# Delta-rule attention ahead of an expert layer and a spectral mixer: loads planned by bytes, zeroing by DMA, filler products and a new order

## The chip, the cores and the metric

The kernel runs on one core of a Trainium2 chip. The metric is the device time of one execution in microseconds (us); the median of three runs is given. The engines are TensorE (PE, whose weight loads are listed as PEld), VectorE (DVE), ScalarE (ACT), GpSimd (POOL) and SyncE (SP), which here only issues transfers. Every engine works through its own instructions in the order of the program and waits at semaphores for the others.

## What is computed

Three layers follow each other for 2 batches of 768 tokens. The first is a recurrent attention (delta rule) with 8 heads of 48 values; its state is updated token by token:

```python
for t in range(S):
    y[:, :, t] = np.einsum('bhd,bhde->bhe', q[:, :, t], state)
    v_old = np.einsum('bhde,bhd->bhe', state, kt)
    state = state + bt[:, :, :, None] * np.einsum('bhd,bhe->bhde', kt, vt - v_old)
```

Here `kt` is the key divided by its norm. The second layer sends each token through one of 8 experts (384 to 1024 to 384 values), chosen by its logits and a local gate. The third adds the real part of a two-dimensional Fourier transform, normalizes, and adds a two-layer network (384 to 1536 to 384). Results have to be close to fp32, so most products are made from fp16 pairs (a high part and a low part), three products for one.

## The kernel before, in words

The program has four stretches: attention (`Attn.run`), routing (`Rest.route`), the experts (`moe_main`) and the mixer. Only the first is touched. `consts_attn` gives it one packed tensor of constants, `ca`.

**Attention.** The 768 tokens are cut into 24 chunks of 32, and 4 chunks make a part `hf` (0 to 5); two parts make a group `g` (0 to 2). For each part there are: `prepK` (L284), which scales the keys by their norms (L291), splits them into a high and a low fp16 buffer (`parts`, L214: L224 on ACT, L243 on DVE or L234 to L238 on PE and ACT), transposes both (`turn`, L164: on PE with a copy by ACT or DVE, or by a DMA), copies the transposed keys into stacked form (`stack`, L313, four copies per part by DVE or ACT as the table `SA` says) and multiplies keys by keys (`gram`, L331); `prepT` (L399) splits the group's solved matrix, spreads it into the block buffers TB (L359 or L362) and multiplies it by the keys (products `wps`, evicted at L421 and L423); `prepV` (L426) splits the values; `prepQ` (L442) splits and spreads the queries (L457, L459, four copies at L466), multiplies them by the keys, masks them (L483) and spreads the result into the block buffers MB. For each group `solve` (L364) inverts a triangular matrix on DVE alone: a stream transpose (L380), 31 pairs of dependent steps (L389, L391) and a transpose of the result, PT (L395). `chain` (L506) carries the recurrent state through the 24 chunks, once for each of two halves of the heads; a step takes products on PE, an eviction on ACT (L531), the low part on DVE or ACT (`low`, L553), the state's eviction on ACT (L548) and its low part `sl` on DVE (`state`, L570). `out` (L576) makes the output of a chunk, `logits` (L620) and `logits_end` (L639) the router's logits from it. When the last parts are ready, `rest` (L670) frees one pool and issues the first expert weights.

**The order.** All of this is written as generators that ask for an engine with a planned time: `yield ("V",929)` asks for DVE for 929 ns. `Order` (L47) is a planner that runs while the program is built. It gives an engine to the request with the smallest priority number (table `PR`, L681; chain and loads have 0) and writes the instructions in that order; `KEEN` and `SHARE` let an engine stay idle a little for an urgent request that is due. Nothing is reordered on the chip. Where two engines can do an operation, `pick` (L59) takes the one that would be done first by the plan, with the corrections of `BIAS` (L680). `dma` (L156) takes SP's queue at 475 ns for an issue, or POOL's at 1081 ns plus `BIAS[6]`, whichever is sooner; in the run shown all loads of attention are issued by SP. `arrive` (L161) says after how many ns from its issue the plan counts a load as landed: a fixed 1850, 2700 or 2900, whatever is queued ahead of it. `LOADS` (L682) is the order of the loads: keys of the first half, constants `c`, `beta`, values, keys of the second half, gate weights `w`, values. The queries' loads (`load_q`, L150) have a priority of their own and fall between them.

**Zeroing.** Twelve fp16 buffers of 128x2048 (QT, TB and MB, two high and two low each) must be zero outside the blocks that are written later, and so must the paddings of the key buffers and the U buffers. `clear` (L195) asks for these as memsets of DVE or POOL (`zero`, L206) with the priorities `CLEAR` (L205).

**TensorE's clock.** `tv` (L491) can put filler products ahead of its own (table `STIRS`, L667), but the table is empty.

Of the kernel before, what the change touches and what calls it, by code (L numbers as in the profile page):

```python
# [6 lines left out]
F32 = mybir.dt.float32  # L7
F32R = mybir.dt.float32r
F16 = mybir.dt.float16
# [13 lines left out]
def consts_attn():  # L23
    c={}
    m=np.zeros((128,32),np.float32)
    for p in range(128): m[p]=(np.arange(32)>(p%32))
    hm=np.zeros((128,2),np.float32)
    for p in range(128): hm[p,(p//32)%2]=SC
    c["ca"]=np.concatenate([hm,m,np.eye(128,dtype=np.float16).view(np.float32),(SC*np.eye(128)).astype(np.float16).view(np.float32),np.eye(128,dtype=np.float32),(-np.eye(128)/SC).astype(np.float16).view(np.float32)],1)
    return c  # L30

def layout(n,a):
# [14 lines left out]
class Order:  # L47
# [3 lines left out]

    LAT={"T":200,"A":160,"V":130,"P":100,"Q":0}
    def __init__(s, keen, share, ticks=None, **res):
        s.KEEN,s.SHARE,s.ticks=keen,share,ticks; s.res=dict(res); s.flags={}; s.wait={}; s.free={}; s.q={}; s.due={}; s.heap=[]; s.n=0; s.now=0
    def add(s,gen,pr=0):
        s.push(s.now,(gen,pr,None))
    def push(s,t,x):
# [6 lines left out]
    def grant(s,e):  # L64

        q=s.q.get(e)
        if not q or s.free.get(e,0)>s.now: return
        pr,_,g,y=q[0]
        s.due[e]=[d for d in s.due.get(e,[]) if d[0]>s.now]
        if any(p<pr and p<=s.KEEN and t<s.now+s.SHARE*y[1] for t,p in s.due[e]): return  # L70
        heapq.heappop(q)
        n=y[1]
        if e=="T" and s.ticks is not None:

            t=(s.now+s.ticks["phase"])//3413; s.ticks[t]=s.ticks.get(t,0)+n
            if s.ticks.get(t-1,0)<1280: n*=2
        s.free[e]=s.now+n
        if "H" in y:

            h=max(s.now,s.free.get("H",0)); s.free["H"]=h+457; s.free[e]+=h-s.now  # L80
        s.push(s.free[e],e)
        s.pr=pr
        n=next(g,None)
        if n is None: return
        t=s.now if 0 in y else s.free[e]+(s.LAT[e] if n[0]!=e or e in "VP" else 0)
        if isinstance(n,tuple) and n[0] in s.LAT: s.due.setdefault(n[0],[]).append((t,pr))
        s.push(t,(g,pr,n))
# [32 lines left out]
class Attn:  # L120
    NB,KP=5,1
    def __init__(s, tc, wk, pk, K, I, q,k,v,beta, xd, lg, psA, psC, psS, late, after):
        s.tc,s.nc,s.wk,s.pk,s.K=tc,tc.nc,wk,pk,K
        s.I,s.lg,s.late,s.after=I,lg,late,after
        s.src={"kp":k,"qp":q,"vp":v}
        s.beta,s.xd=beta,xd
        s.psA,s.psC,s.psS=psA,psC,psS
        s.betaU=pk.tile([128,3,32],F32,name="betaU")
        def zt(n,cnt,sh=[128,16,128],p=wk): return [p.tile(sh,F16,name=f"{n}{i}") for i in range(cnt)]

        s.KBh,s.KBl=[zt(n+"a",1)+zt(n,s.NB-2,p=pk)+zt(n+"b",1) for n in ("KBh","KBl")]
        s.QTs=[zt(f"QT{j}",2) for j in range(2)]
        s.TBh,s.TBl,s.MBh,s.MBl=zt("TBh",2),zt("TBl",2),zt("MBh",2),zt("MBl",2)
        s.Ub=[[zt(f"U{b}{i}",3,[128,2,2,48]) for i in range(2)] for b in range(2)]
        s.L={}; s.KT={}; s.QT={}; s.WT={}; s.V={}; s.G={}; s.P={}; s.PT={}; s.sm={}; s.ST={}
        s.ups=[None]*2; s.S=[None]*2; s.sp={}; s.yb=[None]*2
        s.left={}; s.SB={}; s.STIR=dict(s.STIRS)
        s.o=Order(s.KEEN,s.SHARE,{"phase":0},kp=s.KP,qp=2,vp=1,KT=2,QT0=1,QT1=1,V=2,TB0=1,TB1=1,MB0=1,MB1=1,WT=2,ST=1,ga=2,G=1,P=1,PT=1,SQ=1,am=1,ph=1,u=2,y=2,xT=1,xc=2,yb=3)
    def drop(s,name,key,n=2):

# [3 lines left out]
    def load(s,nm,g):  # L144
        yield ("+",nm)
        t=s.L[nm,g]=s.pk.tile([128,12,4,48],F32,tag=nm,name=nm,bufs=s.KP if nm=="kp" else 1)
        for i in range(3):
            yield from s.dma(t[:,4*i:4*i+4].rearrange("p c q e -> p (c q e)"),s.src[nm][g,:,768*i:768*i+768])
            s.o.add(s.arrive(f"{nm}{3*g+i}",2700))
    def load_q(s):  # L150
        for hf in range(6):
            yield ("+","qp")
            t=s.L["qp",hf]=s.pk.tile([128,1024],F32,tag="qp",name="qp",bufs=2)
            yield from s.dma(t,s.src["qp"][hf])
            s.o.add(s.arrive(f"qp{hf}",2900))
    def dma(s,out,in_,n=475):  # L156

        e=s.o.pick(("Q",n),*(("A",n+35+s.BIAS[5]),)*(s.o.now<s.BOTH),*(("P",1081+s.BIAS[6]),)*(s.o.now<s.THREE))
        yield {"Q":("Q",n,"H"),"A":("A",n+35,"H"),"P":("P",1081)}[e]
        {"Q":s.nc.sync,"A":s.nc.scalar,"P":s.nc.gpsimd}[e].dma_start(out=out,in_=in_)  # L160
    def arrive(s,f,t=1850):  # L161
        yield ("",t)
        yield ("!",f)
    def turn(s,out,in_,f,pe):  # L164

# [18 lines left out]
            yield ("-","y")  # L184
        yield ("!",f)
    def load_beta(s):
        yield from s.dma(s.betaU.rearrange("p g t -> p (g t)"),s.beta)
        s.o.add(s.arrive("beta"))
    def load_consts(s):
        yield from s.dma(s.K["ca"],s.I["ca"])  # L190
        s.o.add(s.arrive("consts"))
    def load_gates(s):
        for t,a in s.late: yield from s.dma(t,a)
        s.o.add(s.arrive("wg"))
    def clear(s):  # L195
        t=s.pk.tile([128,1],F32,tag="one",name="one",bufs=1)
        s.nc.vector.memset(t,1.0)
        s.nc.scalar.activation(out=t,in_=t,func=AF.Sqrt)
        word=lambda t: t.bitcast(F32)
        pad=lambda t: word(t).rearrange("p u (s e) -> p (u s) e",s=2)[:,:,24:32]  # L200
        rows=[(f"K{i}",[pad(s.KBh[i]),pad(s.KBl[i])],(165,260)) for i in range(s.NB)]+[(f"Q{i}",[word(s.QTs[j][i]) for j in range(2)],(912,950)) for i in range(2)]
        rows+=[("U",[t for b in range(2) for i in range(2) for t in s.Ub[b][i]],(107,195))]
        rows+=[(f"{n}{i}",[word(h[i]),word(l[i])],(912,950)) for i in range(2) for n,h,l in (("T",s.TBh,s.TBl),("M",s.MBh,s.MBl))]
        for f,ts,c in rows: s.o.add(s.zero(f,ts,c),s.CLEAR.get(f,9))
    CLEAR={"K0":-1,"K1":0,"Q0":5,"Q1":7,"U":5}  # L205
    def zero(s,f,ts,c):  # L206
        for t in ts:
            e=s.o.pick(("V",c[0]),("P",c[1]))
# [282 lines left out]
    def tv(s,b,c):  # L491
        hf,cc=c//4,c%4; i=hf%2; u0=4*cc+2*b
        if cc==0:
            yield f"V{hf}"
            yield f"T{hf}"
        V=s.V[hf]
        x=s.ups[b]=s.psC.tile([128,2,2,48],F32,tag="u",name="ups",bufs=2)
        for _ in range(s.STIR.pop(c,0)): s.nc.tensor.matmul(out=s.SB[0][:,256:512],lhsT=s.K["identh"],rhs=s.K["idents"],start=False,stop=True,skip_group_check=True)
        yield ("T",255)
        for Q in range(2):  # L500
            u=u0+Q
            s.mm3(x[:,:,Q],[s.TBh[i][:,u],s.TBl[i][:,u]],[V[j][:,u].unsqueeze(1).to_broadcast([128,2,48]) for j in range(2)],Q==0)
        if cc==3:
            yield from s.drop("V",hf)
            yield from s.drop(f"TB{hf%2}",hf)
    def chain(s,b):  # L506
        nc,wk,o=s.nc,s.wk,s.o
# [4 lines left out]
        for c in range(24):  # L512
            hf,cc=c//4,c%4; u0=4*cc+2*b; kb=hf%s.NB
            x=s.ups[b]
# [18 lines left out]
            o.add(s.out(b,c,uh,ul),1)  # L533
            if c<23:
                if c==0:
                    s.SB[b]=s.psS.tile([128,512],F32,tag=f"S{b}",name="S",bufs=1)
                    s.S[b]=s.SB[b][:,0:192].rearrange("p (q a e) -> p q a e",q=2,a=2)
                for n,(st,mv) in enumerate(((s.KBh,uh),(s.KBl,uh),(s.KBh,ul))):
                    if n==0: yield ("T",169)
# [80 lines left out]
    def logits(s,b,hf,yb):  # L620
# [9 lines left out]
        x=s.wk.tile([128,512],F32,tag="xlT",name="xlT",bufs=1)[0:96]  # L630
        yield ("A",478)
        nc.scalar.activation(out=x.rearrange("p (h c t) -> p c h t",h=4,c=4),in_=ps[0:96].rearrange("p (c h t) -> p c h t",h=4,t=32),func=AF.Copy)
        yield ("T",880)
        for h in range(4): nc.tensor.matmul(out=ps[:,0:9],lhsT=x[:,128*h:128*h+128],rhs=s.K["wgq"][:,h],start=(h==0),stop=(h==3))
        yield ("-","xT")
        yield ("A",110)
# [2 lines left out]
    def logits_end(s,b,c,yb):  # L639
# [24 lines left out]
        yield ("!",f"lg{b}{c}")  # L664
        yield ("-","xc")
        yield ("-","ga")
    STIRS={}  # L667
    LOW=(0, 0, 1, 1, 1, 1)
    SA=((0, 0, 0, 0), (0, 0, 0, 0), (0, 1, 1, 0), (0, 1, 0, 1), (1, 0, 0, 0), (0, 0, 1, 1))
    def rest(s):  # L670

        for f in ("ku3","G5","PT2","W43","W53","V4","V5","M4","M5"): yield f
        yield from s.after(s.o)
    BOTH=0
    KEEN,SHARE=2,0.15
    LATE=4
    THREE=30000
    HOLD=(1, 1, 0, 0, 0, 1)
    TK=(1, 1, 0, 0, 0, 0)
    BIAS=(-972, 0, 0, 0, 0, 0, 431, 102)  # L680
    PR={'K0': 0, 'T0': 8.83, 'V0': 28.94, 'Q0': 8.02, 'K1': 4.23, 'T1': 11.55, 'V1': 9.27, 'Q1': 11.93, 'K2': 14.91, 'T2': 2.11, 'V2': 0, 'Q2': 3.47, 'K3': 0.56, 'T3': 11.35, 'V3': 15.56, 'Q3': 8.68, 'K4': 17.19, 'T4': 0, 'V4': 8.5, 'Q4': 9.96, 'K5': 0.49, 'T5': 11.58, 'V5': 7.5, 'Q5': 25.12, 's0': 5.7, 's1': 4.09, 's2': 8.02, 'n0': 1.43, 'n1': 28.97, 'n2': 14.57, 'lq': 7.97, 'lv': 22.18}  # L681
    LOADS="k0 c b v0 k1 w v1"  # L682
    def run(s):
        o=s.o
        s.clear()
        P=lambda n,d: s.PR.get(n,d)
        def loads():
# [863 lines left out]
```

## Time and profile before

| What | us |
|---|---|
| three runs | 580.58, 582.45, 583.3 |
| median | 582.45 |
| the profiled execution | 585.4 |
| its span, first to last instruction | 583.6 |
| DVE busy in the span | 410.7 (70%) |
| PE busy in the span | 490.0 (84%) |

The span is what the profile shows of one execution; 1.8 us of the profiled execution's time lie outside it. Busy shares are means over stretches with different limits, so they are read stretch by stretch: attention runs from 0 to about 244 us, routing to 255, the experts to about 394 and the mixer to the end. The granted clock of TensorE is given as a share of 2.4 GHz; 0.50 is the lower of its two levels.

### The profile page before, as it was taken

To read this page: it belongs to the slowest core of one execution; us is meant where nothing else is said; L and a number is where in the kernel's file an instruction comes from. 1 tells how busy PE (TensorE), PEld (TensorE's weight loads), DVE (VectorE), ACT (ScalarE), POOL (GpSimd) and SP (SyncE) were. 2 spreads that over 40 slices of the span, in tenths; PEclk is the share of its full clock that TensorE was granted. 3 is DMA by queue.
4 is the path that set the end of the run, shared out by engine and by line. 5 is a ranking of instruction groups with operands and counts; after the bars stand their busy time and mean duration, and the time that the engine had idled before them with its cause. 6 is when DMAs were issued, how large, how long until landed. Compare 5 with 4: busy or idle time off the path is not lost.

```text
span 583.6 us, 12586 instructions
## 1 busy us (share of the span) xinstructions
PE 490.0 (84%) x5008; PEld 388.2 (67%) x5008; DVE 410.7 (70%) x918; ACT 332.7 (57%) x769; POOL 77.0 (13%) x81
## 2 busy tenths in 40 slices
PE   0572448884988889769999999999899999999997
PEld 0462147774878778668888888888787655555575
DVE  7969989889994866469888979878987642231132
ACT  3776558995795878836676767672454442111111
POOL 6000000000000000031343322124111210000010
PEclk9986669995895899969999999999999999999999
DMA  7135330766014103829999997328100000010010
GB/s 249 37 51 141 73 73 2 208 98 123 3 28 73 30 2 91 302 60 340 385 323 328 334 300 261 126 67 271 56 2 2 28 1 0 2 55 0 1 55 27
DMA packets 66990, 67.25 MB, mean 115 GB/s; under 512 B 40086, under 2 KB 59483, under 8 KB 66928
## 3 DMA queue, kind: packets, MB, share of 16 engines
q1 hardware_dynamic: 64080, 58.15, 33.4%
q0 software_dynamic: 2848, 8.27, 4.2%
q8 instruction: 40, 0.66, 0.5%
q14 instruction: 22, 0.18, 0.1%
HBM read 51.98 MB, written 7.67 MB: 102 GB/s over the span
## 4 chain that ended last, share of the span: by engine, by line
PE 32%; issue 8%; DVE 7%; DMA 5%; ACT 3%; POOL 1%; SPq 0%; POOLq 0%; ACTq 0%; DVEq 0%
PE mp L1396 12%; PE mop L1422 12%; DMA raw<-moe_w 4%; PE hp L941 3%; DVE ws L917 2%; PE op L953 2%; PE fp L1262 1%; DMA x<-moe_w_ch 1%; PE yp L1231 1%; POOL x2d L962 1%; PE up L1343 1%; ACT ws L914 1%; DVE d L1150 1%; DVE zl L1215 0%; DVE e L1150 0%
## 5 line engine op out<-in xcount | busy, mean ns | idle before, releaser
L1406 DVE SCALAR_TENSOR_TENSOR ml<-mp,mh 128x256 f16<-128x256 f32 (+1 forms) x48 | 26.8, 557 | 81.0 <-ACT mh L1404 80.9
L1396 PE MATMUL mp<-uT,ws 128*128 128x256 f16 (+1 forms) x432 | 77.8, 326 | 0.0
L1422 PE MATMUL mop<-ws,mh 128*128 128x384 f16 x288 | 77.7, 326 | 0.0
L1404 ACT ACTIVATE mh<-mp 128x256 f16<-128x256 f32 (+1 forms) x48 | 23.5, 489 | 89.8 <-PE mp L1396 89.6
L953 PE MATMUL op<-ws,hh 128*128 128x384 f16 (+1 forms) x256 | 67.5, 326 | 0.0
L941 PE MATMUL hp<-xT,ws 128*128 128x240 f16 x576 | 64.8, 266 | 1.0 <-DVE xT L932 0.7
L941 PEld LDWEIGHTS <-ws 128*128 128x128 f16 x576 | 56.2, 98 | 7.2 <-issue 1.5
L1396 PEld LDWEIGHTS <-ws 128*128 128x128 f16 x432 | 42.2, 98 | 27.2
L917 DVE SCALAR_TENSOR_TENSOR ws<-raw,ws 128x1536 f16<-128x1536 f32 x32 | 55.9, 1749 | 0.0
L914 ACT ACTIVATE ws<-raw 128x1536 f16<-128x1536 f32 x32 | 47.3, 1486 | 0.0
L1422 PE MATMUL mop<-ws,ml 128*128 128x384 f16 x144 | 46.9, 326 | 0.0
L953 PE MATMUL op<-ws,hl 128*112 128x384 f16 (+1 forms) x128 | 41.7, 326 | 0.0
L1422 PEld LDWEIGHTS <-mh 128*128 128x128 f16 x288 | 28.2, 98 | 17.8
L330 PEld LDWEIGHTS <-KT 128*128 128x128 f16 x576 | 26.6, 115 | 19.8 <-issue 8.8
L924 POOL DMA_INDIRECT xg<-xd,gm x16 | 22.2, 1389 | 126.8 <-DVE sim L870 120.2
L953 PEld LDWEIGHTS <-hh 128*128 128x128 f16 (+1 forms) x256 | 29.1, 114 | 11.6
L391 DVE TENSOR_TENSOR P<-P,tmp 128x31 f32<-128x31 f32 (+15 forms) x93 | 31.6, 339 | 1.9
L389 DVE TENSOR_TENSOR tmp<-Gu,P 128x31 f32<-128x31 f32 (+15 forms) x93 | 31.3, 336 | 1.9
L962 POOL DMA_INDIRECT x2d<-ot,sim x16 | 19.8, 1238 | 87.5 <-ACT ot L958 85.1
L944 DVE SCALAR_TENSOR_TENSOR hl<-hp,hh 128x480 f16<-128x480 f32 x32 | 20.9, 654 | 14.8 <-ACT hh L943 13.2
L330 PE MATMUL ga<-ST,KT 128*128 128x64 f16 x288 | 16.5, 229 | 17.4 <-DVE ST L326 10.0
L943 ACT ACTIVATE hh<-hp 128x480 f16<-128x480 f32 x32 | 18.1, 567 | 20.6 <-PE hp L941 19.5
(285 smaller groups left out, 1212.4 us busy)
## 6 DMA issues: line engine op xcount, KB each, us to landing
raw<-moe_w SPq DMA_DIRECT2D x64, 384.0 KB
x<-moe_w_ch SPq DMA_DIRECT2D x24, 384.0 KB
qp<-q SPq DMA_DIRECT2D x6, 512.0 KB
kp<-k SPq DMA_DIRECT2D x6, 384.0 KB
vp<-v SPq DMA_DIRECT2D x6, 384.0 KB
xd<-yb SPq DMA_DIRECT2D x48, 48.0 KB
xa<-x2d SPq DMA_DIRECT2D x6, 384.0 KB
ur<-x2d SPq DMA_DIRECT2D x2, 768.0 KB
```

The lines of the kernel that those rows point to most:

```text
L330: s.nc.tensor.matmul(out=out,lhsT=st[l],rhs=mv[m],start=(first and i==0),stop=True,skip_group_check=True)
L389: nc.vector.tensor_tensor(out=x,in0=Gu[:,k,k+1:32].unsqueeze(2).to_broadcast([128,m,n]),in1=P[:,k,0:n].unsqueeze(1).to_broadcast([128,m,n] ...
L391: nc.vector.tensor_tensor(out=P[:,k+1:32,0:n],in0=P[:,k+1:32,0:n],in1=x,op=ALU.subtract)
L914: s.nc.scalar.activation(out=s.W[q][:,0].rearrange("p s c -> p (s c)"),in_=s.raw[q],func=AF.Copy,scale=WS)
L917: s.nc.vector.scalar_tensor_tensor(out=W[1],in0=s.raw[q],scalar=WS,in1=W[0],op0=ALU.mult,op1=ALU.subtract)
L941: nc.tensor.matmul(out=p[:,i],lhsT=s.W[q][:,a,i,128*k:128*k+128],rhs=xT[b][:,k],start=(n==0),stop=(n==8)); n+=1
L953: nc.tensor.matmul(out=s.po[t][0:w],lhsT=hs[a][:,i,128*t:128*t+w],rhs=s.W[q][:,b,i,384:768],start=(g==0 and i==0 and n==0),stop=(g==3 and ...
L962: i=s.nc.gpsimd.indirect_dma_start(out=s.x2d,out_offset=bass.IndirectOffsetOnAxis(ap=s.si[0:w,c:c+1],axis=0),in_=ot,in_offset=None,bounds_ ...
L1396: for k in range(3): nc.tensor.matmul(out=p,lhsT=s.w_ch1(a,k,f),rhs=s.uT[g][b][:,k,0:N],start=(n==0),stop=(n==8)); n+=1
L1404: nc.scalar.activation(out=hh,in_=p,func=AF.Relu)
L1406: nc.vector.scalar_tensor_tensor(out=hl,in0=p,scalar=0.0,in1=hh,op0=ALU.max,op1=ALU.subtract)
L1422: nc.tensor.matmul(out=pm[t],lhsT=hs[a][:,128*t:128*t+128],rhs=s.w_ch2(b,f),start=(f==0 and n==0),stop=(f==11 and n==2))
```

## The change

- A zero tensor of 128x1024 fp32 is a new input. The twelve large buffers (`ZD`) are filled from it by DMA, once the constants have landed by the plan; the paddings and U stay memsets. `CLEAR` has new priorities.
- `arrive` counts a load as landed by bytes: a link that is busy until `s.link` takes 2850 ns per MB, and 1600 ns are added.
- `beta` is loaded ahead of the constants.
- A filler product is a 128x128 by 256-column fp16 product of a zeroed tile `rest0` into an unused half of a PSUM bank. 40 stand ahead of everything, and `STIRS` puts others ahead of PE's turns of the given numbers (a turn is a grant of PE by the plan): 69 in turns 2 to 25, 39 at turn 35, 14 in turns 43 to 78 and 14 in turns 345 to 370. `STIRP` puts 9 products of 128x128 fp32 on PT of group 0 ahead of turn 39.
- `PR`, `KEEN`, `LATE` (the priority of `logits`), `SA` and `BIAS` have new values; `SA` now gives 11 of the 24 stacking copies to ACT (7 before), and `BIAS[6]`, POOL's correction as an issuer of loads, goes from 431 to 0.

```diff
+    c["zero"]=np.zeros((128,1024),np.float32)
...
+        if e=="T":
+            s.turns+=1
+            if s.stir: s.stir(s.turns)
...
-            yield from s.dma(t[:,4*i:4*i+4].rearrange("p c q e -> p (c q e)"),s.src[nm][g,:,768*i:768*i+768])
-            s.o.add(s.arrive(f"{nm}{3*g+i}",2700))
+            yield from s.dma(t[:,4*i:4*i+4].rearrange("p c q e -> p (c q e)"),s.src[nm][g,:,768*i:768*i+768],kb=0.393)
+            s.o.add(s.arrive(f"{nm}{3*g+i}"))
...
+        s.link=max(s.link,s.o.now)+2850*kb
-    def arrive(s,f,t=1850):
-        yield ("",t)
+    def arrive(s,f,t=None):
+        yield ("",s.link-s.o.now+1600 if t is None else t)
         yield ("!",f)
...
-        for f,ts,c in rows: s.o.add(s.zero(f,ts,c),s.CLEAR.get(f,9))
-    CLEAR={"K0":-1,"K1":0,"Q0":5,"Q1":7,"U":5}
+        for f,ts,c in rows: s.o.add(s.zero_dma(f,ts) if f in s.ZD else s.zero(f,ts,c),s.CLEAR.get(f,9))
+    def zero_dma(s,f,ts):
+        yield "consts"
+        for t in ts: yield from s.dma(t.rearrange("p u e -> p (u e)"),s.I["zero"],kb=0.524)
+        s.o.add(s.arrive("0"+f))
+    ZD=("Q0","Q1","M0","M1","T0","T1")
+    CLEAR={'K0': 15.0, 'K1': 13.3, 'Q0': 16.4, 'M0': 20.6, 'Q1': 7.0, 'M1': 0.9, 'U': -0.5, 'K2': 10.9, 'T0': 23.9, 'K3': 22.6, 'K4': 17.6, 'T1': 7.9}
...
-    STIRS={}
+    STIRS={0: 40, 2: 12, 5: 17, 7: 5, 10: 4, 15: 2, 17: 6, 19: 9, 22: 6, 23: 3, 25: 5, 35: 39, 43: 6, 57: 5, 78: 3, 345: 3, 357: 3, 363: 5, 370: 3}
+    def stir(s,k):
+        for _ in range(s.STIRS.get(k,0)):
+            s.nc.tensor.matmul(out=s.SB[0][:,256:512],lhsT=s.rest0[:,0:128],rhs=s.rest0,start=s.fresh,stop=True,skip_group_check=True)
+            s.fresh=False
+        g,n=s.STIRP.get(k,(0,0))
+        if n:
+            x=s.PT[g][:,0:4].rearrange("p a b -> p (a b)")
+            for _ in range(n): s.nc.tensor.matmul(out=s.SB[0][:,256:384],lhsT=x,rhs=x,start=False,stop=True,skip_group_check=True)
+    STIRP={39: (0, 9)}
...
-    SA=((0, 0, 0, 0), (0, 0, 0, 0), (0, 1, 1, 0), (0, 1, 0, 1), (1, 0, 0, 0), (0, 0, 1, 1))
+    SA=((0, 0, 0, 0), (0, 0, 0, 0), (0, 1, 1, 1), (1, 1, 1, 1), (1, 1, 0, 0), (0, 0, 1, 1))
...
-    KEEN,SHARE=2,0.15
-    LATE=4
+    KEEN,SHARE=5,0.15
+    LATE=20
...
-    BIAS=(-972, 0, 0, 0, 0, 0, 431, 102)
-    PR={'K0': 0, 'T0': 8.83, 'V0': 28.94, 'Q0': 8.02, 'K1': 4.23, 'T1': 11.55, 'V1': 9.27, 'Q1': 11.93, 'K2': 14.91, 'T2': 2.11, 'V2': 0, 'Q2': 3.47, 'K3': 0.56, 'T3': 11.35, 'V3': 15.56, 'Q3': 8.68, 'K4': 17.19, 'T4': 0, 'V4': 8.5, 'Q4': 9.96, 'K5': 0.49, 'T5': 11.58, 'V5': 7.5, 'Q5': 25.12, 's0': 5.7, 's1': 4.09, 's2': 8.02, 'n0': 1.43, 'n1': 28.97, 'n2': 14.57, 'lq': 7.97, 'lv': 22.18}
-    LOADS="k0 c b v0 k1 w v1"
+    BIAS=(-972, 0, 970, -319, 0, -211, 0, 287)
+    PR={'K0': 2.56, 'T0': 23.74, 'V0': 19.15, 'Q0': 15.58, 'K1': 6.73, 'T1': 19.9, 'V1': 17.03, 'Q1': 15.71, 'K2': 17.58, 'T2': 4.09, 'V2': 21.01, 'Q2': 7.44, 'K3': 26.4, 'T3': 5.71, 'V3': 8.22, 'Q3': 10.75, 'K4': 40.15, 'T4': 0, 'V4': 16.23, 'Q4': 13.72, 'K5': 3.39, 'T5': 14.94, 'V5': 10.68, 'Q5': 30.12, 's0': 48.55, 's1': 6.77, 's2': 7.72, 'n0': 13.85, 'n1': 13.43, 'n2': 14.57, 'lq': 11.03, 'lv': 8.76}
+    LOADS="k0 b c v0 k1 w v1"
...
+        o.stir=s.stir
+        for b in range(2): s.SB[b]=s.psS.tile([128,512],F32,tag=f"S{b}",name="S",bufs=1)
+        s.rest0=s.pk.tile([128,256],F16,name="rest0")
+        s.nc.gpsimd.memset(s.rest0,0.0)
+        s.stir(0)
         s.clear()
```

## Rows read from the trace of the kernel before

**Rows 1.** The page, part 2: granted clock of TensorE in 40 slices of 14.6 us.

```profile
PEclk9986669995895899969999999999999999999999
```

**Rows 2.** The chain that ended last: start us, us, what (its first piece, its last).

```profile
255.48 1.21 issue
...
579.22 1.05 DVE ur L1430 x2
```

**Rows 3.** Busy time by stretch: us, engines with instructions, PEclk, DMA share, GB/s.

```profile
core 0: us, PE busy (x) PEld busy (x) DVE busy (x) ACT busy (x) POOL busy (x), PEclk, DMA share, GB/s
0.00:78.50 78.50, 31.72 (x365) 24.38 (x366) 67.45 (x163) 46.83 (x75) 9.19 (x23) 0.83 0.45 116
78.50:194.50 116.00, 91.17 (x1476) 83.82 (x1474) 97.56 (x255) 93.62 (x298) 1.90 (x2) 0.82 0.33 67
194.50:244.00 49.50, 44.12 (x769) 40.31 (x765) 29.02 (x81) 40.53 (x144) 0.00 (x0) 0.93 0.35 112
244.00:584.00 340.00, 323.00 (x2414) 239.67 (x2411) 216.61 (x419) 151.72 (x254) 65.93 (x56) 0.98 0.39 132
```

**Rows 4.** DVE in order of time: start us, us, line, operation.

```profile
42.73 1.97 DVE L380 STREAM_TRANSPOSE Gu<-G 128x1024 f32<-128x1024 f32 x1
...
77.23 1.25 DVE L395 STREAM_TRANSPOSE PT<-P 128x1024 f32<-128x1024 f32 x1
...
132.06 1.25 DVE L395 STREAM_TRANSPOSE PT<-P 128x1024 f32<-128x1024 f32 x1
...
193.20 1.25 DVE L395 STREAM_TRANSPOSE PT<-P 128x1024 f32<-128x1024 f32 x1
```

**Rows 5.** All engines in order of time, first 24 us.

```profile
3.10 0.45 SPq L160 DMA_DIRECT2D ca<-ca  x1
...
4.17 0.84 ACT L264 ACTIVATE sq<-kp 128x768 f32<-128x768 f32 x1 [1.95 <-DMA kp<-k]
...
8.85 0.89 DVE L280 TENSOR_SCALAR nsm<-nsm 128x16 f32<-128x16 f32 x1
...
13.71 1.75 ACT L224 ACTIVATE KBha<-kp,ca 128x768 f16<-128x768 f32 x2
...
23.04 0.18 DVE L280 TENSOR_SCALAR nsm<-nsm 128x32 f32<-128x32 f32 x1
```

**Rows 6.** DVE and ACT by line, 0 to 255 us: xcount | busy us, mean ns | idle.

```profile
L326 DVE COPY ST<-KT 64x1024 f16<-64x1024 f16 x17 | 7.1, 419 | 1.1 <-ACT KT L180 0.7
...
L210 DVE MEMSET QT<- 128x1024 f32 x3 | 2.7, 912 | 0.5 <-issue 0.5
...
L210 DVE MEMSET MBh<- 128x1024 f32 x1 | 0.9, 912 | 0.2 <-issue 0.2
...
L323 ACT ACTIVATE ST<-KT 64x1024 f16<-64x1024 f16 x7 | 7.3, 1048 | 2.1 <-DMA KT<-KBl 1.5 <-DMA KT<-KBh 0.5
```

**Rows 7.** Busy time by stretch, columns as in rows 3.

```profile
5.00:10.00 5.00, 0.00 (x0) 0.00 (x0) 4.58 (x13) 0.23 (x2) 4.72 (x10) 1.00 1.02 351
20.00:25.00 5.00, 3.08 (x47) 2.81 (x46) 4.35 (x12) 3.31 (x6) 0.00 (x0) 1.00 0.00 0
```

**Rows 8.** PE in order of time, and one PE group by line.

```profile
23.06 2.61 PE L330 MATMUL ga<-ST,KT 128*128 128x64 f16 x46 [0.84 <-DVE ST L326]
...
42.73 1.56 PE L330 MATMUL ga<-SQ,KT 128*128 128x64 f16 x48
...
82.46 0.27 PE L330 MATMUL wps<-TBh,KBha 128*128 128x128 f16 x1 [3.15 <-DVE TBh L359]
...
L769 PE MATMUL wp<-ca 128*128 128x128 f32 x8 | 2.1, 438 | 0.0
```

**Rows 9.** DVE in order of time, and DVE's wait in total.

```profile
184.17 0.62 DVE L574 SCALAR_TENSOR_TENSOR sl<-S,sh 128x192 f16<-128x192 f32 x2 [4.12 <-ACT sh L548]
...
189.73 0.36 DVE L574 SCALAR_TENSOR_TENSOR sl<-S,sh 128x192 f16<-128x192 f32 x1 [2.54 <-ACT sh L548]
...
DVE sl L574 <- ACT sh L548: 18.8, 18, 4.1
```

More of the change, by code (lines that the diff above doesn't have):

```diff
@@ L53, in __init__ @@
     def __init__(s, keen, share, ticks=None, **res):
-        s.KEEN,s.SHARE,s.ticks=keen,share,ticks; s.res=dict(res); s.flags={}; s.wait={}; s.free={}; s.q={}; s.due={}; s.heap=[]; s.n=0; s.now=0
+        s.KEEN,s.SHARE,s.ticks=keen,share,ticks; s.res=dict(res); s.flags={}; s.wait={}; s.free={}; s.q={}; s.due={}; s.heap=[]; s.n=0; s.now=0; s.turns=0; s.stir=None
     def add(s,gen,pr=0):
@@ L136, in __init__ @@
         s.ups=[None]*2; s.S=[None]*2; s.sp={}; s.yb=[None]*2
-        s.left={}; s.SB={}; s.STIR=dict(s.STIRS)
+        s.left={}; s.link=0; s.SB={}; s.fresh=True
         s.o=Order(s.KEEN,s.SHARE,{"phase":0},kp=s.KP,qp=2,vp=1,KT=2,QT0=1,QT1=1,V=2,TB0=1,TB1=1,MB0=1,MB1=1,WT=2,ST=1,ga=2,G=1,P=1,PT=1,SQ=1,am=1,ph=1,u=2,y=2,xT=1,xc=2,yb=3)
@@ L153, in load_q, with dma @@
             t=s.L["qp",hf]=s.pk.tile([128,1024],F32,tag="qp",name="qp",bufs=2)
-            yield from s.dma(t,s.src["qp"][hf])
-            s.o.add(s.arrive(f"qp{hf}",2900))
-    def dma(s,out,in_,n=475):
+            yield from s.dma(t,s.src["qp"][hf],kb=0.524)
+            s.o.add(s.arrive(f"qp{hf}"))
+    def dma(s,out,in_,n=475,kb=0):
         e=s.o.pick(("Q",n),*(("A",n+35+s.BIAS[5]),)*(s.o.now<s.BOTH),*(("P",1081+s.BIAS[6]),)*(s.o.now<s.THREE))
@@ L186, in load_beta @@
     def load_beta(s):
-        yield from s.dma(s.betaU.rearrange("p g t -> p (g t)"),s.beta)
+        yield from s.dma(s.betaU.rearrange("p g t -> p (g t)"),s.beta,kb=0.05)
         s.o.add(s.arrive("beta"))
     def load_consts(s):
-        yield from s.dma(s.K["ca"],s.I["ca"])
+        yield from s.dma(s.K["ca"],s.I["ca"],kb=0.18)
         s.o.add(s.arrive("consts"))
     def load_gates(s):
-        for t,a in s.late: yield from s.dma(t,a)
+        for t,a in s.late: yield from s.dma(t,a,kb=0.05)
         s.o.add(s.arrive("wg"))
@@ L497, in tv @@
         x=s.ups[b]=s.psC.tile([128,2,2,48],F32,tag="u",name="ups",bufs=2)
-        for _ in range(s.STIR.pop(c,0)): s.nc.tensor.matmul(out=s.SB[0][:,256:512],lhsT=s.K["identh"],rhs=s.K["idents"],start=False,stop=True,skip_group_check=True)
         yield ("T",255)
@@ L535, in chain @@
                 if c==0:
-                    s.SB[b]=s.psS.tile([128,512],F32,tag=f"S{b}",name="S",bufs=1)
                     s.S[b]=s.SB[b][:,0:192].rearrange("p (q a e) -> p q a e",q=2,a=2)
@@ L632, in logits @@
         nc.scalar.activation(out=x.rearrange("p (h c t) -> p c h t",h=4,c=4),in_=ps[0:96].rearrange("p (c h t) -> p c h t",h=4,t=32),func=AF.Copy)
-        yield ("T",880)
+        yield ("T",950)
         for h in range(4): nc.tensor.matmul(out=ps[:,0:9],lhsT=x[:,128*h:128*h+128],rhs=s.K["wgq"][:,h],start=(h==0),stop=(h==3))
```

## The prediction

> **What bounds the kernel now.** I read the chain of waits first. Its pieces begin at 255.48 us, behind attention and routing, and run to the end of the span [rows 2]. So the chain says nothing of the stretch that the change touches. What it does say is that everything behind 255 us follows from its own beginning: if attention ends earlier or later, the 340 us behind it [rows 3] move with it as a block. The first expert weights are issued by attention's own last step, so they move too.
>
> Attention is read from busy time by stretch, cut where DVE finishes the solves [rows 3, 4]. The three PT transposes start at 77.23, 132.06 and 193.20 us and take 1.25 us each; the chain of a part can't start before its PT. Up to 78.5 us DVE is busy for 67.45 us and idle for 11.05. From there to 194.5 it is busy for 97.56 of 116 us, idle for 18.44. Behind that DVE has slack (29.02 of 49.5), and ACT (40.53) and PE (44.12) carry the tail. So attention is a DVE problem up to the last solve, and a problem of latencies between ACT and PE behind it. Time is won by taking work off DVE before 194.5 us, by filling DVE's waits, or by a shorter tail.
>
> TensorE's granted clock falls toward half between about 44 and 88 us, again at 131 to 146 and at 175 to 190 us [rows 1], each time where PE has little to do. The column reads 0.9 or more at the very start, but the instructions say otherwise: at 23.06 us 46 products of 64 columns take 2.61 us, 57 ns each; at 42.73 us 48 of the same size take 1.56 us, 33 ns each [rows 8]. That is the lower level (1.2 GHz) before, the upper (2.4 GHz) after.
>
> **Term A, up to the first PT: -7.9 us.** Six large memsets leave DVE, 3 QT and three alike: 6 x 0.912 = 5.5 us [rows 6]. `SA` moves three stacking copies of parts 2 and 3 from DVE to ACT: 3 x 0.42 = 1.3 us, for 3 x 1.05 us on ACT [rows 6], which has 31 us free there (46.83 of 78.5 busy [rows 3]). DVE's busy time falls from 67.45 to 60.7. What matters is whether its idle time grows by as much. At the start it does: the first keys are there at 4.17 us [rows 5], and the memsets filled the wait for them. Against that, part 0's key split starts at 13.71 us on ACT [rows 5], behind memsets, values and squares that the old order put first. A DVE step of 16 columns took 0.89 us at 8.85 us where one of 32 took 0.18 at 23.04 [rows 5]; POOL was busy with memsets for 4.72 of the 5 us from 5 to 10 [rows 7]. The new floor is the constants' landing. They are now behind three keys, two queries and beta: 2.46 MB, of which the first 0.39 are there at 4.17, so an estimate of 4.17 + 2.07/0.351 = 10.1 us at the 351 GB/s of rows 7, or 3.6 us before 13.71. I take idle time as about 10 us in place of 11: PT at 60.7 + 10 = 70.6 instead of 78.5. The bounds: 0, if all the freed time turns into waiting, and -13, if idle falls to 5, which is the wait for the first keys plus one latency.
>
> The twelve zeroings become transfers: 6.3 MB, 17.9 us at 351 GB/s. They cost nothing if they lie in the gap that the link has from about 13 us on (nothing moves from 20 to 25 us [rows 7]). Each costs SP an issue of about 0.45 us (the constants' [rows 5]), 5.4 us together; behind them on SP stand the later query loads and the transposes by DMA, none of which the trace issues before 24 us. The cover is gone if the plan wants part 0's queries spread before the zeros land.
>
> **Term B, from the first to the last PT: -3.7 us.** One stacking copy of each of parts 4 and 5 goes to ACT, and the first falls here: -0.4. Between 180 and 190 us DVE waits 4.12 and 2.54 us for `sl`'s input [rows 9], in the slices where the clock is low [rows 1]. The 14 fillers at turns 345 to 370 and a new order aim there. Bounds 0 and -6.7; the half, -3.3, since nothing before shows either how a filler or how the order acts.
>
> **Term C, the tail: -1 us.** LATE=20 moves router products behind the chain's; what is left to do at the end may also grow. Bounds +3 and -5, by DVE's and ACT's idle time of 20.5 and 9 us there [rows 3]; I take -1.
>
> **Term D, fillers in the way: +1 us.** By the pitch of rows 8 a 256-column product costs 4 x 57 = 227 ns at the lower level, 4 x 33 = 130 at the upper. The 40 first ones (5 to 9 us) run while PE has no work, and the 39 at turn 35 (5.1 to 8.9 us) have PE's idle time up to the first PT as cover: 78.5 - 31.7 = 47 us [rows 3]. If one of them stands before ready work, everything on PE waits, and ACT's evictions and DVE's copies behind it. The nine fp32 products at turn 39 add a wait: PE can't pass them before PT of group 0 is there. Queued behind are the `wps` products, which wait for PT anyway. PE stood 3.15 us there [rows 8]; nine at 2.1/8 = 0.26 us make 2.4 us, inside that gap. The gain is the `wps` products at the upper level. Bounds 0 and +8.9; near 0 for the gap's sake, so +1, with the early products' gain set against it.
>
> **Sum.** -7.9 - 3.7 - 1 + 1 = -11.6 us, against the profiled execution's 585.4, which is 2.95 over the median 582.45. Against the median: 570.9, so 571.
>
> A rule speaks against a part of this: the Trainium skill, page "SBUF — State Buffer", section "SBUF: two separate sides", says that a transfer issued by GpSimd gets no descriptors while VectorE holds the port that the two share. With `BIAS[6]` at 0 the plan may give POOL some zeroings. The slow step at 8.85 us [rows 5] shows the two engines in each other's way, though with a memset; no row here shows a GpSimd transfer in attention. By that rule the zeros land late, which is the second rival below.
>
> **The rivals.**
> 1. *More than half of the waits go.* DVE's idle time up to the last PT is 29.5 us, and if the new plan, made with landings that are nearer to rows 7, brings it down by 12 instead of 4, and the clock's part goes too, the sum is about -22: 560 us. For it: loads that were planned at a fixed time came later, and DVE stood. Against it: many of the waits are short and follow from the chain's latency.
> 2. *The zeros or later loads land late.* All of term A's DVE time turns into waiting at the first copy into QT: -11.6 + 7.9 = -3.7, about 579. For it: 17.9 us of new traffic, in order on one queue. Against it: the idle link of rows 7.
> 3. *A plan that waits more, slower than before.* DVE works in the written order; it waits for `sl` 18 times, 18.8 us in all [rows 9], because chain steps came later than planned. If the new order weaves chain and solves tighter and its plan is no truer, these waits double at the same place, between 88 and 194 us: -11.6 + 18.8 = +7.2, 590 us. It decides from 11.6 us of additional waiting. For it: most of the priorities are new at once, and each depends on planned times. Against it: the landings are planned closer to the trace.
> 4. *The fillers stand before ready work* at turn 35 and in turns 2 to 25: all of +8.9 in place of +1, 579 us.
>
> **How the numbers follow.** The main case has 0.45, rival 1 has 0.2, rival 2 has 0.12, rival 3 has 0.17, rival 4 has 0.06. The range goes from 557 (rival 1 with 3 us more of the tail) to 589, which takes in the bounds of the main case (571 - 13 and 571 + 12) and leaves out about half of rival 3. Within 0.5%, about what can be told from no change here, is 579.5 to 585.4. Faster gets nearly all of the main case and rival 1 and half of rivals 2 and 4: 0.71. Slower is rival 3 without its mild forms: 0.16. The rest is 0.13.
>
> **What the profile of the changed kernel would show.** Right: the first PT near 70 us, the last near 183, attention's end near 232, no 128x1024 memsets on DVE, and the stretch behind unchanged at 340 us. Part 0's split at about 10 us would bear out the start. A wait of DVE for the zeros at its first QT copy would show rival 2, a larger sum of waits for `sl` rival 3, PE busy with fillers while DVE or ACT waits for PE rival 4. The clock column should no longer fall before the first `wps`. I would be wrong altogether if the stretch behind 255 us changed its length, for instance by weights issued later against attention's end.

## The result, and the profile after

The kernel after takes 585.31 us (median of 8 runs, 584.13 to 586.69), the kernel before beside it 582.22 (8 runs, 580.15 to 584.11): a ratio of 1.0053, interval 1.0031 to 1.0076. It is slower by half a per cent, where 571 us was forecast. The two profiled executions lie closer, 584.41 after and 585.4 before, since that of before was 3 us over its median. Two executions among all runs below were far longer than the rest of their kernel (753 us of the kernel after, 1009 us of one variant), and the ratios leave them out.

The page of the kernel after: span, granted clock by slices, and the group of the fp16 fillers.

```profile
span 582.6 us, 12967 instructions
...
PEclk8786589997699799869999999999999999999999
...
L679 PE MATMUL S<-rest 128*128 128x256 f16 x176 | 25.3, 296 | 2.8 <-DVE sl L582 1.7
```

Busy time of the kernel after by stretch, columns as in [rows 3], cut where its solves end.

```profile
0.00:78.00 78.00, 42.90 (x468) 33.81 (x469) 61.67 (x158) 46.43 (x75) 5.69 (x19) 0.76 0.59 190
78.00:192.00 114.00, 88.28 (x1528) 80.37 (x1527) 99.77 (x262) 92.34 (x288) 1.90 (x2) 0.91 0.34 73
192.00:243.00 51.00, 46.08 (x797) 42.59 (x793) 31.45 (x93) 42.30 (x145) 0.00 (x0) 0.93 0.26 73
243.00:584.00 341.00, 323.84 (x2409) 240.42 (x2409) 216.85 (x416) 150.17 (x252) 65.15 (x56) 0.98 0.40 137
```

DVE of the kernel after in order of time: the transposes that answer to [rows 4], and the first step of routing.

```profile
43.68 1.95 DVE L390 STREAM_TRANSPOSE Gu<-G 128x1024 f32<-128x1024 f32 x1
...
78.00 1.25 DVE L405 STREAM_TRANSPOSE PT<-P 128x1024 f32<-128x1024 f32 x1
...
137.10 1.24 DVE L405 STREAM_TRANSPOSE PT<-P 128x1024 f32<-128x1024 f32 x1
...
190.42 1.25 DVE L405 STREAM_TRANSPOSE PT<-P 128x1024 f32<-128x1024 f32 x1
...
242.40 0.25 DVE L796 TENSOR_REDUCE mx<-lg 128x12 f32<-128x96 f32 x1
```

DVE's work up to the first PT did fall: to 61.67 us of 78.0, and to 62.9 of 79.25 with the PT transpose itself, where it was 67.45 of 78.5 [rows 3]. Its idle time grew instead, from 11.05 to 16.3 us, and the first PT didn't come earlier: 78.00 against 77.23. From the first to the last PT it is 112.42 us against 115.97. From routing's first step (at 244.39 in the kernel before) to the end of the span it is 340.2 us against 339.2, so the block behind kept its length within 1 us. Most of what is missing of the forecast sits ahead of the first PT, and the start shows a part of it.

All engines of the kernel after in order of time, first 14 us (SPq and POOL rows are issues of transfers).

```profile
3.54 0.46 SPq L164 DMA_DIRECT2D ca<-ca  x1
...
3.89 0.71 POOL L164 DMA_DIRECT2D MBh<-zero  x1
...
5.67 0.55 POOL L164 DMA_DIRECT2D MBl<-zero  x1
...
11.49 0.20 DVE L384 TENSOR_SCALAR P<-betaU 128x32 f32<-128x32 f32 x1 [2.14 <-DMA betaU<-beta]
...
13.28 0.93 ACT L234 ACTIVATE KBha<-kp,ca 128x768 f16<-128x768 f32 x1 [5.23 <-DMA ca<-ca]
```

The plan gave POOL four of the twelve zeroings. "Once the constants have landed" holds in the plan alone: nothing on the chip waits for it, and POOL, with nothing else to do, issues them from 3.89 us on, right behind the constants' own issue on SP at 3.54. The first key split on ACT then stands 5.23 us for the constants. In the kernel before it began at 13.71 behind other work of ACT [rows 5].

Transfers of the kernel after in its first 20 us: packets, MB and share of each queue; then issues, KB each, median us from issue to landing.

```profile
q1 hardware_dynamic: 1738, 4.75, 66.2%
q0 software_dynamic: 576, 2.10, 25.9%
...
QT<-zero SPq DMA_DIRECT2D x3, 512.0 KB, 12.1
...
MBl<-zero POOLq DMA_DIRECT2D x2, 512.0 KB, 10.8
...
MBh<-zero POOLq DMA_DIRECT2D x1, 512.0 KB, 7.5
QT<-zero POOLq DMA_DIRECT2D x1, 512.0 KB, 10.8
...
ca<-ca SPq DMA_DIRECT2D x1, 177.0 KB, 9.7
```

POOL's queue moved 2.10 MB beside SP's 4.75. POOL's four zeroings of 0.5 MB, issued behind the constants, landed after 7.5, 9.1, 10.8 and 12.6 us; the 177 KB of constants, issued before them, needed 9.7.

### The profile page after: what moved, and what is told of

It is laid out like the page before. It is cut to its first block, busy times and chain, and to the rows that moved or that the text cites. A ratio compares the mean times of both kernels' runs of the same rounds, so it can differ in the third digit from the quotient of the medians.

```text
span 582.6 us, 12967 instructions
## 1 busy us (share of the span) xinstructions
PE 501.1 (86%) x5196; PEld 397.2 (68%) x5196; DVE 409.7 (70%) x926; ACT 331.3 (57%) x758; POOL 72.7 (12%) x77
## 4 chain that ended last, share of the span: by engine, by line
PE 34%; DVE 8%; issue 5%; DMA 4%; ACT 2%; POOL 0%; SPq 0%; ACTq 0%; DVEq 0%; POOLq 0%
PE mp L1419 12%; PE mop L1445 12%; PE hp L964 3%; PE op L976 3%; DVE ws L940 3%; DMA x<-moe_w_ch 2%; PE fp L1285 2%; DVE dec L932 1%; PE yp L1254 1%; DMA xa<-x2d 1%; DVE hl L967 1%; ACT hh L966 1%; DMA raw<-moe_w 1%; PE up L1366 1%; ACT ws L937 1%
## 5 line engine op out<-in xcount | busy, mean ns | idle before, releaser
L340 PEld LDWEIGHTS <-KT 128*128 128x128 f16 x576 | 24.4, 107 | 15.5 <-issue 11.3
L679 PE MATMUL S<-rest 128*128 128x256 f16 x176 | 25.3, 296 | 2.8 <-DVE sl L582 1.7
```

The costliest lines, as they stand in the source:

```text
L340: s.nc.tensor.matmul(out=out,lhsT=st[l],rhs=mv[m],start=(first and i==0),stop=True,skip_group_check=True)
L679: s.nc.tensor.matmul(out=s.SB[0][:,256:512],lhsT=s.rest0[:,0:128],rhs=s.rest0,start=s.fresh,stop=True,skip_group_check=True)
```

## The experiments

Two theories follow from these rows: POOL's zeroings hold up the constants, and the fillers stand before ready work. A third, that DVE's memsets had only filled waits, would say that the forecast gain was never there. The first PT of one kernel moves by about 1 us between executions (78.00 and 78.80 in two traces of after, 77.23 and 76.34 in two of before) and later places move by more, so small differences go by the medians. The kernel before took 583.13, 583.34 and 583.33 us in the three batches.

**The kernel after again**, unchanged, on the chip of the next three.

> The changed kernel once more, on the chip of the three runs below, as their point of comparison: 1.005 of the kernel before, part 0's key split at 13.3 us behind the constants, the first PT transpose at 78, the last at 190.4, attention's end near 242. If these times move by more than 1 us from one execution to the next, single traces can't tell the effects below.

585.48 us, 1.0024 [1.0005, 1.0044]: slower than before again. First PT 78.80, last PT 195.06, routing from 244.74. The last PT is 4.6 us behind that of the first trace, well over the 1 us of the expectation, so at that place a single trace can't tell effects of a few us.

**Without fillers.**

```diff
-    STIRS={0: 40, 2: 12, ...}
+    STIRS={}
-    STIRP={39: (0, 9)}
+    STIRP={}
```

> All filler products are left out (they compute nothing that is used); every engine's other instructions keep their order. Theory 'fillers in the way': the twelve fillers at 16.65 us no longer hold up the low-part transposes (19.2 us becomes about 17), and the first PT comes 2 us earlier, the time falls by 2 us. Rival 'the fillers pay': the products behind the first PT and near 180 us run at the lower level, the last PT comes 3 us later and the time rises by 2 to 4 us. Rival 'DVE bound': nothing moves by more than 1 us.

582.19 us, 0.9981 [0.9960, 1.0003]: 3.3 us less than after. First PT 79.30, no earlier; from there to the second solve's Gu 10.1 us instead of 12.0 and 12.8 in the two traces of after. So the fillers cost something, behind the first PT, and the new order without them is still no faster than before.

**The four zeroings of POOL issued by SP**, at their place in the order, plan untouched.

```diff
-        {"Q":s.nc.sync,"A":s.nc.scalar,"P":s.nc.gpsimd}[e].dma_start(out=out,in_=in_)
+        (s.nc.sync if in_ is s.I["zero"] else {"Q":s.nc.sync,"A":s.nc.scalar,"P":s.nc.gpsimd}[e]).dma_start(out=out,in_=in_)
```

> The four zeroings that POOL issues (at 3.9 to 6.2 us) are issued by SP instead, in the same place of the plan and so behind the loads of keys, beta, constants and values; the rest keeps its order. Theory 'the zeros took the link from the constants': the constants land at 10 us in place of 13.3, the key split starts there, the first PT comes 3 us earlier (75), the time falls by 2 to 3 us. Rival 'DVE bound': the split starts earlier and the first PT stays within 1 us of 78. Rival 'zeros late': DVE waits at its first QT copy, and the first PT is later than 78.

581.54 us, 0.9962 [0.9942, 0.9982]: 3.9 us less than after. The first key split begins at 10.48, the first PT at 74.86, 3.1 and 3.9 us earlier than in the two traces of after.

**Both.**

> Both at once: no fillers, and all zeroings issued by SP. If the two losses are real and independent, the first PT comes 5 us earlier than 78 and the time falls by 4 to 5 us against the changed kernel. If both are waits for the same thing, the gain is that of the larger alone. If the fillers pay, it is worse than the run with SP's zeroings alone.

578.77 us, 0.9911 [0.9898, 0.9925]: 6.7 us less than after, where the two alone gave 3.3 and 3.9. They add up.

All engines of this kernel in order of time: the first key split, the first solve's ends, and the place behind the first PT.

```profile
10.18 0.94 ACT L234 ACTIVATE KBha<-kp,ca 128x768 f16<-128x768 f32 x1 [2.44 <-DMA ca<-ca]
...
40.46 1.94 DVE L390 STREAM_TRANSPOSE Gu<-G 128x1024 f32<-128x1024 f32 x1
...
75.04 1.25 DVE L405 STREAM_TRANSPOSE PT<-P 128x1024 f32<-128x1024 f32 x1
...
79.46 1.33 PE L340 MATMUL ga<-ST,KT 128*128 128x64 f16 x22 [3.44 <-ACT ST L333]
...
81.55 0.31 PE L340 MATMUL wps<-TBh,KBha 128*128 128x128 f16 x1
...
85.15 1.94 DVE L390 STREAM_TRANSPOSE Gu<-G 128x1024 f32<-128x1024 f32 x1
```

The same place with SP's zeroings and all fillers.

```profile
74.86 1.25 DVE L405 STREAM_TRANSPOSE PT<-P 128x1024 f32<-128x1024 f32 x1
...
81.60 3.56 PE L684 MATMUL S<-PT 128*128 128x128 f32 x18
...
85.00 0.22 PE L340 MATMUL wps<-TBh,KBha 128*128 128x128 f16 x1
...
87.50 1.95 DVE L390 STREAM_TRANSPOSE Gu<-G 128x1024 f32<-128x1024 f32 x1
```

The nine fp32 products (18 records, 3.56 us) start where the `wps` products began without them. These come 3.45 us later, at the upper level (a pitch of about 56 ns instead of 106), and the next solve's Gu 2.35 us later. The fillers ahead of the first PT left no mark on it: 74.86 with them, 75.04 without.

**All but the fp32 products**: SP's zeroings, all fp16 fillers, `STIRP={}`.

> SP's zeroings and all fp16 fillers, only the nine fp32 products on PT are left out. Theory 'the nine stand before ready work': products behind the first PT start 3.4 us earlier than with them, the second solve starts about 2.4 us earlier after the first PT (10.1 us in place of 12.6), and the time is that of the run without any filler, 0.991. Rival 'the 39 or the early ones cost it': it stays at 0.996.

577.36 us, 0.9908 [0.9884, 0.9931]. That is 4.2 us less than with them by the medians of two batches, 3.1 by the ratios. The second solve's Gu comes at 85.05, 10.1 us behind the first PT, as the theory had it. Against no fillers at all it is 1.4 us less, and the intervals overlap: the 176 fp16 fillers are worth nothing that these runs can tell. This kernel is faster than the kernel after, and 1% faster than the kernel before. In its trace routing starts at 235.48.

**Only the later fp16 fillers**, and **only those up to turn 35**, otherwise as the last kernel.

```diff
+    STIRS={43: 6, 57: 5, 78: 3, 345: 3, 357: 3, 363: 5, 370: 3}
...
+    STIRS={0: 40, 2: 12, 5: 17, 7: 5, 10: 4, 15: 2, 17: 6, 19: 9, 22: 6, 23: 3, 25: 5, 35: 39}
```

> SP issues the zeroings, no fp32 products, and of the fp16 fillers only those of turns 43 and later (14 + 14 + the 9 between, 37 minus none: 43, 57, 78, 345, 357, 363, 370) are left. Without any filler (e3) attention ended at 238.4 us and the run took 578.8; with all fp16 ones (e5) 235.5 and 577.4. My theory: the early fillers fill idle time of PE and move nothing, the late ones raise the clock in the tail (186 to 236 us: 0.99 against 0.86), so this run shows the end of attention at 235 to 236.5 and 576 to 577.5 us, the first PT at 75. Rival, the early ones carry the gain (a clock that is already up when the first products come): first PT later than in e5 by 1 us or more, attention's end at 238, 578.8 us.

> SP issues the zeroings, no fp32 products, and of the fp16 fillers only those ahead of everything and of turns 2 to 35 are left. My theory: the early ones move nothing that counts, so attention ends at 238 us as without any (e3), first PT at 75, granted clock of 186 to 236 us back at 0.86, 578.8 us. Rival, the early ones carry the gain: attention's end at 235.5, 577.4 us or less.

577.90 us, 0.9903 [0.9868, 0.9938], and 579.96, 0.9939 [0.9916, 0.9962]. First PT 75.16 and 75.02: the early ones move nothing there, as my theory had it. Routing starts at 237.41, between the places that the two theories gave, and at 240.72, later than either; the two times lie the same way. The granted clock from 186 to 236 us is 0.93 and 0.90, between the 0.86 without fillers and the 0.99 with all fp16 ones. Whether the late ones speed up the tail stays open: the intervals of all four kernels (none, both, late, early) overlap or touch.

**The zeroings as memsets of POOL**, no transfers and no fillers.

```diff
-        {"Q":s.nc.sync,"A":s.nc.scalar,"P":s.nc.gpsimd}[e].dma_start(out=out,in_=in_)
+        if in_ is s.I["zero"]: s.nc.gpsimd.memset(out,0.0)
+        else: {"Q":s.nc.sync,"A":s.nc.scalar,"P":s.nc.gpsimd}[e].dma_start(out=out,in_=in_)
```

> As the run without fillers and with SP's zeroings, but the twelve zeroings are memsets of POOL, in the places where the plan had their transfers: no transfer of zeros at all, 11.4 us of POOL's time from 4 us on. Theory 'the link is the price': the constants land at 10 us as with SP's zeroings, nothing else is gained, 0.991 of the kernel before within 0.003. Rival 'POOL in DVE's way' (the 0.89 us step of the kernel before): small DVE steps between 5 and 16 us are stretched, the first PT comes 1 to 3 us later than 75. Rival 'the zeros on SP still held up the values': the first PT comes 1 to 2 us earlier.

586.19 us, 1.0040 [1.0022, 1.0058], 7.4 us more than the same order with SP's transfers; first PT 81.65. What taking the traffic away is worth can't be told from it, since POOL was in DVE's way. This kernel's engines in order of time:

```profile
5.85 8.83 DVE L281 TENSOR_SCALAR nsm<-nsm 128x16 f32<-128x16 f32 x1
...
13.71 0.94 POOL L164 MEMSET MBl<- 128x1024 f32 x1
14.72 0.21 ACT L283 ACTIVATE nsm<-nsm 128x16 f32<-128x16 f32 x1 [9.89 <-DVE nsm L281]
...
17.16 0.94 ACT L235 ACTIVATE KBha<-kp,ca 128x768 f16<-128x768 f32 x1 [1.49 <-DVE kp L302]
```

A DVE step of 16 columns, 0.17 us at the same place in the kernel with SP's transfers, takes 8.83: it ends at 14.68, when POOL's last memset does (13.71 + 0.94). All of the keys' norms wait behind it.

**The kernel before in its own order, its twelve large memsets as SP's transfers behind the first values.** It asks what DVE's freed time is worth without the new order; POOL's six memsets go, too.

```diff
+            if c[0]==912: s.big.append(t)
+            else: (s.nc.vector if e=="V" else s.nc.gpsimd).memset(t,0.0)
...
+                if n=="v0":
+                    for t in s.big: s.nc.sync.dma_start(out=t.rearrange("p u e -> p (u e)"),in_=s.I["zero"])
```

> The kernel before, its order and plan untouched, only its twelve 128x1024 memsets (six on DVE, six on POOL) are transfers from zeros, issued by SP behind the first values. Theory 'the memsets filled waits': of the 5.5 us taken off DVE next to nothing arrives, the first PT is earlier by 0 to 2 us than 77.2 and the time by 0 to 1.5 us. Rival 'DVE's time counts': the first PT is 5 us earlier, the time 4 to 5 us lower.

581.66 us, 0.9965 [0.9945, 0.9986]: 1.7 us less. First PT 76.04, 0.3 to 1.2 us earlier than in two traces of before (77.23 and 76.34).

**The kernel before again**, one execution on the same chip.

> The kernel before once more with a profile, for a second trace: the first PT at 77.2, the last at 193.2, routing from 244.4 in the trace shown. If these places move by 2 us or more, the trace of one execution says little about differences of this size.

582.63 us; the first solve's Gu at 41.61, the PT transposes at 76.34, 131.24 and 191.24, routing from 242.25. The last PT and routing moved by about the 2 us that the expectation named.

Where DVE's freed time went is read from its busy time by stretch (third number behind the stretch's length). First the kernel before, columns as in [rows 3]:

```profile
0.00:10.00 10.00, 0.00 (x0) 0.00 (x0) 8.26 (x20) 2.54 (x4) 9.19 (x23) 1.00 0.81 279
10.00:20.00 10.00, 3.03 (x26) 2.63 (x27) 7.61 (x14) 7.03 (x9) 0.00 (x0) 1.00 0.21 84
20.00:30.00 10.00, 4.79 (x64) 4.09 (x62) 9.26 (x19) 7.11 (x11) 0.00 (x0) 1.00 0.17 54
30.00:41.00 11.00, 8.72 (x123) 7.71 (x124) 6.67 (x15) 8.25 (x14) 0.00 (x0) 0.90 0.12 39
41.00:76.00 35.00, 13.36 (x124) 8.11 (x121) 33.31 (x92) 21.54 (x39) 0.00 (x0) 0.69 0.57 118
```

The old order with the memsets as SP's transfers:

```profile
0.00:10.00 10.00, 0.00 (x0) 0.00 (x0) 3.27 (x15) 2.55 (x4) 3.81 (x17) 1.00 0.80 280
10.00:20.00 10.00, 3.92 (x32) 3.35 (x33) 7.46 (x15) 8.09 (x11) 0.00 (x0) 1.00 1.03 414
20.00:30.00 10.00, 4.91 (x67) 4.38 (x67) 8.69 (x18) 6.07 (x9) 0.00 (x0) 1.00 0.89 354
30.00:41.00 11.00, 8.69 (x145) 7.44 (x143) 7.70 (x18) 9.33 (x17) 0.00 (x0) 1.00 0.24 61
41.00:76.00 35.00, 11.69 (x108) 7.11 (x105) 33.28 (x93) 20.75 (x36) 0.00 (x0) 0.65 0.57 118
```

Up to 41 us DVE is busy for 31.80 us before and for 27.12 with the memsets gone: 4.7 us of work less, and the solve behind it begins between 0 and 1.1 us earlier (41.61 against 42.73 and 41.61). It came out of the first 10 us (3.27 us busy in place of 8.26). From 41 to 76 us DVE is full in both. What the next steps then stood for is in the rows in order of time, first of the kernel before:

```profile
10.39 0.20 DVE L374 TENSOR_SCALAR P<-betaU 128x32 f32<-128x32 f32 x1 [0.65 <-DMA betaU<-beta]
...
11.27 1.81 ACT L436 ACTIVATE V<-vp 128x768 f16<-128x768 f32 x2 [3.53 <-DMA vp<-v]
```

The old order with the memsets as SP's transfers:

```profile
10.24 0.20 DVE L378 TENSOR_SCALAR P<-betaU 128x32 f32<-128x32 f32 x1 [3.01 <-DMA betaU<-beta]
...
11.09 1.82 ACT L440 ACTIVATE V<-vp 128x768 f16<-128x768 f32 x2 [4.77 <-DMA vp<-v]
...
13.55 1.75 ACT L228 ACTIVATE KBha<-kp,ca 128x768 f16<-128x768 f32 x2
```

DVE gets no further until `beta` is there, and ACT, which has the values ahead of the key split, no further until the values are. Both landings stay within 0.2 us of where they were, and so does the key split (13.55 against 13.71 [rows 5]).

## Why the prediction was wrong

**Term A (-7.9) is the step that failed.** It had DVE's freed time come out whole, on the argument that its idle time stays at 10 us; in the kernel after it is 16.3. Three things stood against that, each with its run. First, the freed time turned into waits. The old order with transfers gains 0.3 to 1.2 us at the first PT for 4.7 us less work, because its next steps stand for `beta` and the values. The new order with all zeroings on SP has the first PT at 74.86 to 75.16 us in five traces, 1.2 to 2.4 us earlier, not 7.9; without fillers DVE is then busy for 62.97 of the 76.3 us to the end of PT, and idle for 13.3. This is nearer to the bound of 0 that I gave ("if all the freed time turns into waiting") than to the -7.9. Second, the constants' landing. My 10.1 us is what the chip gives (10.18) once POOL issues nothing; with POOL's four zeroings it was 13.28, and the first PT came 3.1 to 4.3 us later. I had noted that the plan might use POOL, but had put the zeroings into the gap of the link from 13 us on, where nothing on the chip held them. The third lies behind the first PT and belongs to D.

**Term B (-3.7) came out in one trace of two, by luck.** From the first to the last PT it is 112.42 us in the kernel after and 116.26 in its repeat, against 115.97 and 114.90 in two traces of before. Without the fp32 products it is 110.6 to 110.8 in five traces, and 114.3 in a sixth. How this came about is not that of the text, which hoped for fillers at 180 to 190 us: the kernel without any, and with SP's zeroings, has 110.62, so the order does it. Its parts are others, too. From the first PT to the second solve's Gu it takes 10.1 us, against 5.3 before: the new order puts more of DVE's other steps ahead of that solve. The second solve, from its Gu to its PT, takes 47.2 against 49.5, and the third 47.6 against 55.3. DVE's waits for `sl` are 13.4 us in 21 pieces in the kernel after, against 18.8 in 18 [rows 9]. Rival 3, which let them double, is out, though its 590 lies as near to the result as anything I wrote. The prediction also misread `SA`: one more copy of part 4 goes to ACT and none of part 5; its -0.4 counts one copy and stands.

**Term C (-1)** can't be told: 52.0 us from the last PT to routing against 51.2 and 51.0 in two traces of before, and 49.7 to 52.7 in the other traces of the new order.

**Term D (+1) named the place and mis-sized it.** The nine fp32 products were to fit in the 3.15 us in which PE waited for TB [rows 8]. In the new order that gap isn't there: the `wps` products start at 81.55 without a wait, just where the fillers would. PE does stand still, 3.44 us, but ahead of the `ga` products at 79.46, which come before the fillers' turn. The nine took 3.24 to 3.99 us in three traces, not 2.4. The size came from a row of eight records [rows 8] that was read as eight products. That row is cut by the end of its window; the whole group, from 240 to 262 us in the kernel before, is 20 products (`WARMR`) in 40 records:

```profile
L769 PE MATMUL wp<-ca 128*128 128x128 f32 x40 | 6.6, 343 | 0.0
```

That is 0.33 us a product, or 3.0 us for nine. They cost 2.4 us by the second solve (its Gu at 87.50 against 85.05). By the last PT it is 3.7 (114.30 from the first PT against 110.63), but the run with the early fillers has 114.29 without them, so that the rest is theirs isn't shown. The 39 fillers at turn 35, which I feared more, cost nothing at the second solve: 10.1 us behind the first PT with and without them. For fp16 products the pitches came near: in the kernel after 12 in 2.77 us at 16.65, at the lower level, are 231 ns each (227 forecast), and 39 in 4.42 us at 74.64 are 113 (130 forecast).

**Rival 2** was right that landings decide, wrong in which: not the zeros were late, the constants were. The rule cited for it, from the Trainium skill, page "SBUF — State Buffer", section "SBUF: two separate sides", was that a transfer issued by GpSimd gets no descriptors while VectorE holds the port that the two share. This trace doesn't show such a delay: POOL's zeroings landed in 7.5 to 12.6 us, SP's of the same size in 10.5 to 12.3. The harm went the other way, from POOL's transfers to SP's constants. **Rival 4** was right in kind, but at the fp32 products of turn 39, not at the turns that it named.

The account by medians: 583.1 before; -4.4 for order and transfers with SP alone (578.8), where A, B and C made -12.6 (in the old order the transfers alone gave -1.7); +3.3 for the fillers and +3.4 for POOL's queue (585.5). **What stays open**: why the loads' packets share the link as they do, whether the late fp16 fillers gain 1 us or nothing, and which table of the new order (`PR`, `SA`, `KEEN`, `LATE`, `BIAS`) does what, since no run changes one of them alone.

## What to carry to other kernels

Work that an engine does while nothing else is ready costs little, and taking it away gains little (here 1.7 us by the median, for six memsets of 0.91 us each): ask first what ends the wait that it fills. A wait that exists in a planner alone holds no engine back; look for the semaphore, above all where an otherwise idle engine issues transfers. A filler product belongs where the trace of the new order, not of the old, shows the engine waiting.

## What the runs showed of the hardware

POOL's memsets, back to back, held one DVE step of 16 columns for 8.83 us; a reduction from 128x768 at 4.86 us in the same trace ran beside them in its usual 0.95. The Trainium skill, page "SBUF — State Buffer", section "SBUF: two separate sides", calls the port that the two engines share an exclusive lock, held for a whole instruction. That the step waited fits the lock; but it was passed over by the nine memsets that POOL began after it (6.56 to 13.71 us), where the page lets one expect a wait for the one under way. The slow step of 0.89 us [rows 5] looks like a mild case of it: it ends at 9.74, one memset of POOL at 9.71 (8.77 + 0.94), and in the old order without the large memsets the same step takes 0.17.

The first 40 fillers didn't hold the clock. They ran from 1.10 to 7.32 us, then PE had nothing until 15.83, and in the kernel after the granted clock of the stretch from 10 to 20 us is 0.57; the first eight transposes, at 15.83, took 1.03 us as they did without any filler (1.03 at 16.90):

```profile
10.00:20.00 10.00, 4.17 (x28) 3.43 (x29) 5.25 (x9) 4.07 (x5) 0.00 (x0) 0.57 1.03 407
```

The column alone doesn't show this: it reads 1.00 from 10 to 20 us in the two kernels of the new order without fillers, one with POOL's and one with SP's zeroings, whose first transposes are just as slow. The next 12 fillers did raise the clock. In the run with SP's zeroings and all fp16 fillers, the eight transposes behind them take 0.61 us, at 16.40; without fillers they take 1.01, at 15.56. What the clock gave, the place in line took: the first solve's Gu is at 40.66 with them and 40.46 without.

A part of the spread between traces has a place: from 115 to 125 us the granted clock was 1.00 in seven traces of the new order, but 0.74 in the repeat of after and 0.83 in the run with the early fillers. In these two the solve that runs then, from the second Gu to its PT, took 49.8 and 49.7 us, in the others 47.1 to 47.3. What sets it off was not tried; the first of them had every filler, and the kernel with none had 1.00. Nor is it shown that the clock is the cause: in the old order the same solve takes 49.5 us at a granted clock of 1.00.
